# A fused FFT filter and top-128 FFN: the input laid out in DRAM in the order of the tile's rows, so that half of a batch is two transfers instead of eight

## The chip, the core and the metric

The kernel runs on one core of one Trainium2 chip. It is written in Bass under the Tile framework. The metric is device time in microseconds (us) for one execution. Five engines run their own instruction streams in order: TensorE (PE, matmuls; PEld is its weight load), VectorE (DVE), ScalarE (ACT), GpSimd (POOL) and SyncE (SP). In this kernel SP issues nearly all the transfers between DRAM and on-chip memory (SBUF); 16 DMA engines carry them out.

## The reference, cut to what matters

`x` has 8 batches of 3136 tokens with 256 channels, all in float32. The first half filters each channel along the tokens by a Fourier transform, a product with a complex filter and the inverse transform. The second half scores each token, takes the 128 best of each batch, runs them through a small two-layer network and adds the result, gated, to those tokens.

```
X = np.fft.rfft(x, axis=1)
y = np.fft.irfft(X * (filt_r + 1j * filt_i)[None], n=3136, axis=1)
scores = einsum('bsd,d->bs', y, w_gate); top 128 per batch
out = y;  out[top] += sigmoid(score) * (relu(y[top] @ w1) @ w2)
```

## The kernel before, in words

The 3136 tokens are taken as 98 x 32. A two-stage transform is used: an outer one over the 98 and an inner one over the 32, both as matmuls against constant tables.

The tile `X` has 128 partitions, 32 positions and 256 channels, and there is only one of it. A batch comes in folded for the outer transform: token row `a` (0 to 48) of the first and of the second half of the sequence, and even and odd positions (`w` = 0, 1), so that partitions 0 to 48 hold `w` = 0 and partitions 64 to 112 hold `w` = 1. Rows 49 to 63 belong to no token; the fold reads all 113 rows.

Work on a batch goes through these steps.

- `load` (line 535) brings a half of a batch (128 of the 256 channels) into `X`. For batches 0 and 1 it brings all 256 channels at once. Lines 542 and 545 issue it: four transfers of 48 partitions (first the two for partitions 64 to 111, then the two for partitions 0 to 47) and four of one partition.
- `outer` (line 404) works in 8 chunks of 32 channels, four to a half of `X`. For the batch that comes in, a chunk is folded (sum and difference, line 427, on POOL or DVE, or left to PE as extra matmuls), multiplied on PE (`amm`, line 453) and transposed into `UU` on DVE (line 457). The two letters of a chunk in `FOLD` say who makes the sum and who the difference: `p` POOL, `d` DVE, `x` PE.
- `inner` (line 341) makes the inner transform, the product with the filter and the inner inverse: lines 356 and 365 on PE, 374 and 390 on ACT, 378 on DVE, 381 on POOL.
- For the batch that goes out, `outer` transposes `UU` back on DVE (418), multiplies on PE (511) and copies the result over the same channels of `X` on ACT (514). When the four chunks of a half are done, `store` (533) writes this half to `out` in one transfer of 98 partitions; the last two batches use another path (489 to 498, stored by lines 528 and 531).
- `select` finds the 128 best tokens; it passes its scores through a scratch tensor in DRAM (`scr`, line 600, read back as `R`, line 605).

A half of `X` is thus reused in a fixed cycle: store of batch b, load of batch b + 3, fold and matmul of b + 3 in four chunks, results of batch b + 1 copied in, store of b + 1. While one batch comes in, the one before it is in the inner transform and the one before that goes out.

The order of all this is a list of numbers, `ORDER`, found beforehand with a planner: every step of the program is appended to `prog` by `op`, and the loop at the end issues them in the order of the list. Each engine keeps to that order, and SP too: a transfer is issued only when everything before it on SP has been issued. `PLAN` holds the other choices (`FOLD`, which engine spreads which part of the filter tables, which PSUM bank a matmul uses).

Of the kernel before, what the change touches and what calls it, by code (L numbers as in the profile page):

```python
# [44 lines left out]
def _tables(C):  # L45
# [45 lines left out]
    for r in range(8):  # L91
# [33 lines left out]
    BRING=["aazaaazz", "zvaaavzv", "aavaaaaa", "azvavaaa", "aaaaaaaa", "avzavvaa", "aaaaaaaa", "azvazavz"],  # L125
    SPR=[
        ["dve", "pool", "pool", "act"],
        ["pool", "dve", "pool", "pool"],
        ["dve", "act", "act", "dve"],
        ["dve", "act", "pool", "dve"],  # L130
    ],
    SELM=[0, 0, 0, 0, 0, 0, 0, 1],
    WPOOL=[7, 0, 1],
    PARTS=[(0, 2), (2, 4), (4, 8), (8, 13)],
    ALONE=[["a", "z", "v"], ["a"]],
    TRING=["z", "v", "z", "v"],
# [105 lines left out]
def kernel(  # L242
# [20 lines left out]
    HD = D // 2  # L263
    CW, CY = 32, 16
    DS = D + 1
    xv = x.rearrange("b (h a n w) d -> b w h a n d", h=2, w=2, n=N2 // 2)
    ov = out.rearrange("b (a c) d -> b a c d", c=N2)
    ow = out.rearrange("b (h a n w) d -> b w h a n d", h=2, w=2, n=N2 // 2)
    of = out.rearrange("b s d -> (b s) d")
# [841 lines left out]
```

## Time and profile before

| What | Value |
|---|---|
| median of 3 runs (lowest, highest) | 551.62 us (546.82, 552.71) |
| the profiled execution | 553.32 us, span of its instructions 551.5 us |
| TensorE clock granted in the span | 0.915 of full speed |
| PE busy | 458.5 us (83%) |
| DVE busy | 401.8 us (73%) |
| POOL busy | 291.8 us (53%) |
| ACT busy | 285.0 us (52%) |
| packets of the DMA queue that SP feeds | 103366, 62.53 MB, 61.8% of 16 engines' span |

Times in the rows below count from the first instruction of the profiled execution. A row of the timeline gives start, length, engine, line, operation, what it writes and reads, and in brackets how long its engine sat idle before it and what ended the idle time. [...]

### The profile page before, as it was taken

Reading aid. Unit: us, or ns where it says so; the run is one execution under the profiler, and the core shown is the slowest. Engines: PE = TensorE matmul, PEld = TensorE weight load, DVE = VectorE, ACT = ScalarE, POOL = GpSimd, SP = SyncE. Lnnn points to the kernel's source line nnn. Section 1 sums busy time; section 2 is a strip of 40 time slices with the busy share of each in tenths; the row PEclk is TensorE's granted clock in tenths of the full one; section 3 lists DMA queues with packets and bytes.
Section 4 is the critical chain, followed back from the end, with each engine's and each line's share of the span. In section 5 each row is a group of like instructions: output and inputs, shape, how many; then the busy total and the mean of one; then the engine's idle time right before and its main releaser. Section 6 shows DMA issues by size and latency. Waiting matters only on the chain. (4 is left out here: it accounts for less than half of the span.)

```text
span 551.5 us, 10702 instructions
## 1 busy us (share of the span) xinstructions
PE 458.5 (83%) x3888; PEld 232.9 (42%) x3888; DVE 401.8 (73%) x1016; ACT 285.0 (52%) x708; POOL 291.8 (53%) x236
## 2 busy tenths in 40 slices
PE   4094377799879989989799959996999896999996
PEld 4042153333324433434244415442443353566896
DVE  2086277779968998788579948994798897588642
ACT  1025242146565666458456835784467755776421
POOL 2092277695638735776378637854858334232022
PEclk9576878799999989989989988998899999799999
DMA  9999942860789385928883898289743336247410
GB/s 121 138 260 122 140 98 47 128 92 2 169 146 144 86 161 91 167 50 177 154 126 57 173 178 103 48 174 177 94 67 108 109 85 207 64 114 161 132 40 30
DMA packets 104186, 65.31 MB, mean 118 GB/s; under 512 B 5062, under 2 KB 102470, under 8 KB 103878
## 3 DMA queue, kind: packets, MB, share of 16 engines
q1 hardware_dynamic: 103366, 62.53, 61.8%
q0 software_dynamic: 768, 2.10, 1.2%
q8 instruction: 31, 0.51, 0.4%
q14 instruction: 21, 0.17, 0.1%
HBM read 37.68 MB, written 26.94 MB: 117 GB/s over the span
## 5 line engine op out<-in xcount | busy, mean ns | idle before, releaser
L381 POOL TENSOR_TENSOR q<-q,fb_sb 128x512 f32<-128x512 f32 (+1 forms) x104 | 133.0, 1298 | 82.5 <-ACT q L374 68.3
L427 POOL TENSOR_TENSOR s<-X 113x512 f32<-113x512 f32 x53 | 68.3, 1290 | 106.9 <-DMA X<-in_x_dram 59.7
L511 PE MATMUL py<-t,c_sb 128*98 128x512 f32 x208 | 119.0, 655 | 5.2 <-ACT X L514 3.9
L453 PE MATMUL pa<-X,c_sb 49*64 49x512 f32 x292 | 84.3, 708 | 27.3 <-DMA c_sb<-in_cst_dram 16.5
L396 DVE SCALAR_TENSOR_TENSOR rj<-pv,wg_sb 128x256 bf16<-128x256 f32 x200 | 83.8, 419 | 19.7 <-ACT UU L390 11.2
L457 DVE STREAM_TRANSPOSE UU<-pa 128x1024 f32<-128x1024 f32 x59 | 73.3, 1242 | 18.5 <-PE pa L453 17.8
L514 ACT COPY X<-py 98x512 f32<-98x512 f32 x104 | 60.5, 582 | 47.2 <-PE py L511 15.9
L418 DVE STREAM_TRANSPOSE t<-UU 128x1024 f32<-128x1024 f32 x64 | 78.5, 1229 | 5.3 <-PE py L511 3.7
L453 PE MATMUL pa<-s,c_sb 49*64 49x512 f32 x228 | 66.1, 650 | 18.0 <-POOL s L427 16.5
L374 ACT COPY q<-pz 128x512 f32<-128x512 f32 (+1 forms) x104 | 56.5, 586 | 47.3 <-PE pz L356 46.6
L365 PE MATMUL pv<-y,ti_sb 64*64 64x256 f32 x800 | 70.8, 395 | 11.0 <-DVE rj L396 11.0
L378 DVE TENSOR_TENSOR y<-pz,fa_sb 128x512 f32<-128x512 f32 (+1 forms) x104 | 67.9, 677 | 15.9 <-ACT q L374 13.4
L356 PE MATMUL pz<-UU,tf_sb 64*64 64x256 f32 x800 | 67.4, 426 | 13.2 <-DVE y L378 9.7
L390 ACT COPY UU<-pv 128x512 f32<-128x512 f32 x96 | 51.5, 588 | 46.8 <-PE pv L365 46.5
L365 PE MATMUL pv<-q,ti_sb 64*64 64x256 f32 x800 | 68.4, 384 | 3.0 <-POOL q L381 3.0
L427 POOL TENSOR_TENSOR X<-X 113x512 f32<-113x512 f32 x47 | 60.8, 1294 | 4.0 <-DVE s L427 0.6
L356 PEld LDWEIGHTS pz<-UU,tf_sb 64*64 64x64 f32 x800 | 32.0, 143 | 53.1 <-issue 20.6
L511 PEld LDWEIGHTS py<-t,c_sb 128*98 128x98 f32 x208 | 27.0, 170 | 54.4 <-ACT X L514 20.1
L365 PEld LDWEIGHTS pv<-y,ti_sb 64*64 64x64 f32 x800 | 30.5, 134 | 44.5 <-issue 13.1
L365 PEld LDWEIGHTS pv<-q,ti_sb 64*64 64x64 f32 x800 | 35.1, 136 | 16.3 <-POOL q L381 3.9
L453 PEld LDWEIGHTS pa<-X,c_sb 49*64 49x64 f32 x292 | 19.9, 148 | 40.8 <-issue 31.5
L427 DVE TENSOR_TENSOR s<-X 113x512 f32<-113x512 f32 x6 | 7.3, 1224 | 34.9 <-DMA fa_sb<-in_fri_dram 34.3
(193 smaller groups left out, 598.7 us busy)
## 6 DMA issues: line engine op xcount, KB each, us to landing
out_dram<-X SPq DMA_DIRECT2D x13, 1568.0 KB
X<-in_x_dram SPq DMA_DIRECT2D x48, 384.0 KB
X<-in_x_dram SPq DMA_DIRECT2D x8, 768.0 KB
out_dram<-X SPq DMA_DIRECT2D x12, 384.0 KB
R<-scr SPq DMA_DIRECT2D x16, 196.0 KB
fb_sb<-in_moe_w_dram SPq DMA_DIRECT2D x2, 1024.0 KB
ti_sb<-in_ti_dram SPq DMA_DIRECT2D x1, 832.0 KB
tf_sb<-in_tf_dram SPq DMA_DIRECT2D x1, 800.0 KB
```

The costliest lines, as they stand in the source:

```text
L356: nc.tensor.matmul(half(z, k)[o, hi], lhsT=tf_sb[p, l], rhs=urow(b, l, 0, D)[p], start=True, stop=True)
L365: nc.tensor.matmul(half(v, k)[o, j], lhsT=ti_at[p, t, i, hi], rhs=y[p, hi], start=t == 0, stop=t == 1)
L374: nc.scalar.copy(out=q[:np_], in_=half(h["z"], k)[:np_])
L378: nc.vector.tensor_tensor(out=y[:np_], in0=half(h["z"], k)[:np_], in1=fa_sb[:np_, i], op=ALU.mult)
L381: nc.gpsimd.tensor_tensor(out=h["q", k][:np_], in0=h["q", k][:np_], in1=fb_sb[:np_, i], op=ALU.mult)
L396: nc.vector.scalar_tensor_tensor(out=rj, in0=half(h["v"], k)[:, j], scalar=1.0, in1=wg_sb, op0=ALU.mult, op1=ALU.mult, accum_out=urow(b, l ...
L418: nc.vector.transpose(out=h["t"].rearrange("p d (l j) -> p d l j", j=2), in_=uchan(b_out, c))
L427: (nc.gpsimd if fold[k] == "p" else nc.vector).tensor_tensor(out=out, in0=two[0], in1=two[1], op=(ALU.add, ALU.subtract)[k])
L453: nc.tensor.matmul(a[o, w].rearrange("p (n d) -> p n d", d=CW), lhsT=lhs[p], rhs=rhs[p], start=n == 0, stop=n == len(terms) - 1)
L457: nc.vector.transpose(out=uchan(b_in, c), in_=h["a"].rearrange("p w (n d) -> p d n w", d=CW))
L511: nc.tensor.matmul(yp[:N1], lhsT=cc["wi"][:, :N1], rhs=h["t"][:, n * CY:(n + 1) * CY].rearrange("p a b -> p (a b)"), start=True, stop=True)
L514: nc.scalar.copy(out=X[:N1, :, at], in_=e["y"][:N1])
```

## The change

On the host, `x` is rearranged before the launch into an array of 8 batches x 2 halves of the channels x 113 rows x 32 positions x 128 channels, with zeros in rows 49 to 63. A half of a batch is then 113 rows of 16 KB, one after the other in DRAM, in the order of the tile's partitions. `load` becomes two transfers, one of 112 partitions and one of the last row, for every batch, the first two included. The two memsets that cleared rows 32 to 63 of `X` are gone. `ORDER` is another list, and some choices of `PLAN` differ.

```diff
-    nc.vector.memset(X[32:64, :N2 // 2], 0.0)
-    nc.gpsimd.memset(X[32:64, N2 // 2:], 0.0)
...
     def load(when, b, h, bias=0.0):
         def f():
-            if b >= B or (b < 2 and h == 1):
-                return
-            at = slice(0, D) if b < 2 else slice(h * HD, h * HD + HD)
-            for w in (1, 0):
-                for k in range(2):
-                    nc.sync.dma_start(out=Xh[64 * w:64 * w + 48, k, :, at], in_=xv[b, w, k, :48, :, at])
-            for w in range(2):
-                for k in range(2):
-                    nc.sync.dma_start(out=Xh[64 * w + 48:64 * w + 49, k, :, at], in_=xv[b, w, k, 48:49, :, at])
+            if b < B:
+                at = slice(h * HD, h * HD + HD)
+                nc.sync.dma_start(out=X[:112, :, at], in_=x[b, h, :112])
+                nc.sync.dma_start(out=X[112:RW2, :, at], in_=x[b, h, 112:])
...
+    xs = np.zeros((B, 2, RW2, 2, N2 // 2, D // 2), np.float32)
+    tokens = data["x"].reshape(B, 2, NH, N2 // 2, 2, 2, D // 2)
+    for w in range(2):
+        xs[:, :, 64 * w:64 * w + NH] = tokens[:, :, :, :, w].transpose(0, 4, 2, 1, 3, 5)
+    data["x"] = xs.reshape(B, 2, RW2, N2, D // 2)
...
-        "xx xd xx dp pp xx pp xx",
+        "xp dp pd dx dd pp xx pd",
...
-    1, 3, 0, 4, 2, 10, 35, 37, 46, 5, 47, 38, 42, 43, 11, 50, 6, 36, 39, 44, 15, 12, 48, 13, 51, 20, 40, 14, 52, 53,
```

Over the whole program the counts on the engines hardly differ: PE has two matmuls of `amm` more, DVE four folds more, POOL five fewer, the eight threshold steps of one batch's `select` go from ACT to DVE, and two subtractions of the network's weights from DVE to POOL.

Three places show how the order moves. The first is SP at the start of the program, up to the filter tables. Before:

```order
L542 DMA X<-in_x_dram 48x16x256 x4
L545 DMA X<-in_x_dram 1x16x256 x4
L1021 DMA c_sb<-in_cst_dram 128x192
L976 DMA fa_sb<-in_fri_dram 32x1024 x2
L976 DMA fb_sb<-in_fri_dram 32x1024 x2
L1024 DMA tf_sb<-in_tf_dram 128x1600
```

Now:

```order
L968 DMA fa_sb<-in_fri_dram 32x1024 x2
L968 DMA fb_sb<-in_fri_dram 32x1024 x2
L1013 DMA c_sb<-in_cst_dram 128x192
L536 DMA X<-in_x_dram 112x32x128
L537 DMA X<-in_x_dram 1x32x128
L536 DMA X<-in_x_dram 112x32x128
L537 DMA X<-in_x_dram 1x32x128
L1017 DMA wg_sb<-in_moe_w_gate_dram 128x256
L1016 DMA tf_sb<-in_tf_dram 128x1600
```

The first part of the filter tables (`fa_sb`, `fb_sb`) and the constants of `amm` (`c_sb`) now go ahead of the first batch, and the batch comes as two halves.

The second is SP in the middle of the program, from one store of a first half to the read-back of `select`, in the batch whose first half is stored fourth. Before:

```order
L533 DMA out_dram<-X 3136x1x128
L542 DMA X<-in_x_dram 48x16x128 x4
L545 DMA X<-in_x_dram 1x16x128 x4
L533 DMA out_dram<-X 3136x1x128
L600 DMA scr<-kf 98x2x32
L542 DMA X<-in_x_dram 48x16x128 x4
L545 DMA X<-in_x_dram 1x16x128 x4
L605 DMA R<-scr 128x1x392 x2
```

Now:

```order
L530 DMA out_dram<-X 3136x1x128
L536 DMA X<-in_x_dram 112x32x128
L537 DMA X<-in_x_dram 1x32x128
L592 DMA scr<-kf 98x2x32
L530 DMA out_dram<-X 3136x1x128
L536 DMA X<-in_x_dram 112x32x128
L537 DMA X<-in_x_dram 1x32x128
L597 DMA R<-scr 128x1x392 x2
```

The pair of store and load keeps its place; the scratch write of `select` stands ahead of the second store in this batch and in the two around it, where it stood behind it.

The third is PE at the start, from the first `amm` on (`pa`, `pz` and `pv` are PSUM tiles, `s` is a folded sum). Before:

```order
L453 MATMUL pa<-X,c_sb 64x512 x8
L453 MATMUL pz<-X,c_sb 64x512 x4
L453 MATMUL pz<-s,c_sb 64x512 x2
L453 MATMUL pv<-X,c_sb 64x512 x8
L453 MATMUL pa<-s,c_sb 64x512 x2
```

Now:

```order
L450 MATMUL pa<-X,c_sb 64x512 x8
L450 MATMUL pz<-s,c_sb 64x512 x2
L450 MATMUL pz<-X,c_sb 64x512 x2
L450 MATMUL pv<-s,c_sb 64x512 x2
L450 MATMUL pv<-X,c_sb 64x512 x2
```

The first batch has fewer chunks whose fold is left to PE, and PE begins with a chunk of the half that is loaded first.

## Rows read from the trace of the kernel before

**Rows 1.** The page's 40 slices of the span, 13.8 us each: the granted clock in tenths, and what the DMA engines moved.

```profile
PEclk9576878799999989989989988998899999799999
GB/s 121 138 260 122 140 98 47 128 92 2 169 146 144 86 161 91 167 50 177 154 126 57 173 178 103 48 174 177 94 67 108 109 85 207 64 114 161 132 40 30
```

**Rows 2.** The waits: engine, line and tile that waited, for what, us in total, times, the longest in us.

```profile
POOL s L427 <- DMA X<-in_x_dram: 59.7, 8, 13.4
```

**Rows 3.** The timeline of SP: issues of loads of `X` (L542) and of stores of a half (L533).

```profile
91.39 3.53 SPq L542 DMA_DIRECT2D X<-in_x_dram  x4
...
145.76 3.75 SPq L542 DMA_DIRECT2D X<-in_x_dram  x4
...
198.98 3.35 SPq L542 DMA_DIRECT2D X<-in_x_dram  x4
...
256.24 3.70 SPq L542 DMA_DIRECT2D X<-in_x_dram  x4
...
302.20 0.90 SPq L533 DMA_DIRECT2D out_dram<-X  x1
310.63 3.92 SPq L542 DMA_DIRECT2D X<-in_x_dram  x4
...
357.56 0.90 SPq L533 DMA_DIRECT2D out_dram<-X  x1
366.15 3.34 SPq L542 DMA_DIRECT2D X<-in_x_dram  x4
```

**Rows 4.** The timeline of POOL: the folds that waited for a load of `X`.

```profile
107.29 1.27 POOL L427 TENSOR_TENSOR s<-X 113x512 f32<-113x512 f32 x1 [4.67 <-DMA X<-in_x_dram]
161.25 1.26 POOL L427 TENSOR_TENSOR s<-X 113x512 f32<-113x512 f32 x1 [9.09 <-DMA X<-in_x_dram]
213.94 1.26 POOL L427 TENSOR_TENSOR s<-X 113x512 f32<-113x512 f32 x1 [6.02 <-DMA X<-in_x_dram]
...
270.38 1.25 POOL L427 TENSOR_TENSOR s<-X 113x512 f32<-113x512 f32 x1 [11.36 <-DMA X<-in_x_dram]
325.65 2.46 POOL L427 TENSOR_TENSOR s<-X 113x512 f32<-113x512 f32 x2 [13.43 <-DMA X<-in_x_dram]
...
380.14 1.25 POOL L427 TENSOR_TENSOR s<-X 113x512 f32<-113x512 f32 x1 [12.98 <-DMA X<-in_x_dram]
```

**Rows 5.** Stretches chosen for what the DMA engines carry in them: us, busy time of each engine (with its instructions), granted clock, share of the 16 DMA engines, GB/s. From 4 to 26 the load of batch 0; from 28 to 42 tables; from 359 to 365 a store of 98 partitions; from 368 to 377 one load of 4 transfers of 48 partitions, cut where its rate changes; from 450 to 454 a store as 4 transfers of 48 partitions; from 466 to 469 the network's weights onto 128 partitions, one of the two tensors in pieces of 1 KB.

```profile
4.00:26.00 22.00, 6.83 (x68) 6.69 (x68) 1.13 (x1) 0.20 (x1) 0.44 (x3) 0.72 1.14 140
28.00:42.00 14.00, 14.00 (x100) 6.53 (x100) 11.69 (x11) 3.48 (x3) 12.54 (x10) 0.77 0.89 255
...
359.00:365.00 6.00, 6.00 (x63) 2.75 (x63) 5.60 (x15) 5.02 (x15) 5.68 (x5) 1.00 0.91 257
368.00:369.00 1.00, 0.74 (x9) 0.13 (x2) 0.93 (x5) 0.97 (x4) 0.00 (x0) 1.00 1.10 244
369.00:373.00 4.00, 4.00 (x22) 1.26 (x22) 3.81 (x8) 2.89 (x9) 0.00 (x0) 1.00 1.23 136
373.00:374.00 1.00, 1.00 (x7) 0.41 (x3) 0.97 (x6) 0.26 (x2) 0.00 (x0) 1.00 1.22 195
374.00:377.00 3.00, 2.28 (x21) 0.85 (x20) 2.25 (x3) 2.33 (x7) 0.00 (x0) 1.00 1.25 143
...
450.00:454.00 4.00, 4.00 (x42) 1.85 (x38) 3.82 (x16) 1.89 (x4) 1.91 (x2) 1.00 0.86 182
...
466.00:469.00 3.00, 2.07 (x28) 1.75 (x32) 2.59 (x7) 1.56 (x5) 1.27 (x1) 0.80 1.03 373
```

**Rows 6.** The same view for stretches around the waits of rows 4: the first number after the stretch's length is PE's busy time, the third from the end the granted clock.

```profile
330.00:385.00 55.00, 50.33 (x427) 21.52 (x421) 42.86 (x117) 33.87 (x91) 35.41 (x29) 0.93 0.71 126
...
262.00:274.00 12.00, 8.47 (x48) 2.71 (x42) 7.97 (x17) 6.58 (x20) 3.54 (x3) 0.97 0.85 135
274.00:281.00 7.00, 7.00 (x34) 2.47 (x35) 2.96 (x8) 2.21 (x7) 6.84 (x7) 0.57 0.49 138
316.00:329.00 13.00, 6.99 (x36) 2.05 (x36) 6.28 (x11) 6.16 (x19) 3.27 (x3) 0.96 1.09 198
329.00:336.00 7.00, 7.00 (x43) 2.67 (x43) 2.91 (x8) 2.48 (x8) 6.25 (x6) 0.59 0.12 25
372.00:382.00 10.00, 5.85 (x37) 1.98 (x36) 5.66 (x10) 5.21 (x16) 1.78 (x2) 1.00 1.08 186
382.00:390.00 8.00, 7.49 (x30) 2.20 (x26) 3.35 (x8) 1.82 (x5) 7.84 (x7) 0.57 0.27 79
...
152.00:166.00 14.00, 11.19 (x80) 3.94 (x71) 8.99 (x22) 9.06 (x27) 4.75 (x5) 0.93 0.89 151
...
100.00:111.00 11.00, 7.63 (x38) 3.23 (x42) 7.99 (x20) 1.00 (x4) 6.18 (x6) 0.62 0.77 117
```

**Rows 7.** The timeline at the start: the first `amm`, the first matmul of `inner`, and the first `amm` of batch 1.

```profile
27.92 3.93 PE L453 MATMUL pa<-X,c_sb 49*64 49x512 f32 x16 [16.54 <-DMA c_sb<-in_cst_dram]
...
45.82 1.99 PE L356 MATMUL pz<-UU,tf_sb 64*64 64x256 f32 x16 [3.31 <-DVE UU L457]
...
70.65 4.48 PE L453 MATMUL pa<-X,c_sb 49*64 49x512 f32 x16 [9.34 <-DMA X<-in_x_dram]
```

**Rows 8.** The groups by line: busy us in all, mean ns of one, idle time before them and what ended it.

```profile
L427 POOL TENSOR_TENSOR s<-X 113x512 f32<-113x512 f32 x53 | 68.3, 1290 | 106.9 <-DMA X<-in_x_dram 59.7 <-DMA c_sb<-in_cst_dram 23.3 <-DMA fa_sb<-in_fri_dram 11.6
L427 DVE TENSOR_TENSOR s<-X 113x512 f32<-113x512 f32 x6 | 7.3, 1224 | 34.9 <-DMA fa_sb<-in_fri_dram 34.3 <-POOL s L427 0.7
L284 DVE MEMSET X<- 32x4096 f32 x1 | 3.5, 3472 | 1.7 <-PEq L1100 1.7
```

More of the change, by code (lines that the diff above doesn't have):

```diff
@@ L124 @@
     BACK=["ffffffff", "ffffffff", "ffffffff", "ffffffff", "ffffffff", "ffffffff", "qeqeqqqe", "eeeeffff"],
-    BRING=["aazaaazz", "zvaaavzv", "aavaaaaa", "azvavaaa", "aaaaaaaa", "avzavvaa", "aaaaaaaa", "azvazavz"],
+    BRING=["aazaavza", "vaazvzav", "vazzzaza", "zzavazza", "aaaaaava", "avzvvvaz", "aaaaaaaa", "azvaaaaa"],
     SPR=[
-        ["dve", "pool", "pool", "act"],
-        ["pool", "dve", "pool", "pool"],
-        ["dve", "act", "act", "dve"],
+        ["dve", "act", "pool", "pool"],
+        ["act", "pool", "act", "dve"],
         ["dve", "act", "pool", "dve"],
+        ["act", "act", "pool", "dve"],
     ],
-    SELM=[0, 0, 0, 0, 0, 0, 0, 1],
-    WPOOL=[7, 0, 1],
+    SELM=[0, 0, 0, 0, 0, 1, 0, 1],
+    WPOOL=[4, 5, 0, 1, 7],
     PARTS=[(0, 2), (2, 4), (4, 8), (8, 13)],
     ALONE=[["a", "z", "v"], ["a"]],
-    TRING=["z", "v", "z", "v"],
+    TRING=["z", "z", "v", "z"],
     URING=["m", "v", "v"],
@@ L265 @@
     DS = D + 1
-    xv = x.rearrange("b (h a n w) d -> b w h a n d", h=2, w=2, n=N2 // 2)
     ov = out.rearrange("b (a c) d -> b a c d", c=N2)
@@ L519, in outer @@
             if b_out >= 0 and o + CW == HD:
-                op(t0 + 4.4, "sp", 7.2, lambda hx=hx: store(b_out, hx),
+                op(t0 + 4.4, "sp", 7.2 if back == "f" else 10.5, lambda hx=hx: store(b_out, hx),
                    [("x", hx, c - k) for k in range(HD // CW)], [("out", b_out)], lat=.9)
@@ L536, in f @@
         def f():
-            if b >= B or (b < 2 and h == 1):
-                return
-            at = slice(0, D) if b < 2 else slice(h * HD, h * HD + HD)
-            for w in (1, 0):
-                for k in range(2):
-                    nc.sync.dma_start(out=Xh[64 * w:64 * w + 48, k, :, at], in_=xv[b, w, k, :48, :, at])
-            for w in range(2):
-                for k in range(2):
-                    nc.sync.dma_start(out=Xh[64 * w + 48:64 * w + 49, k, :, at], in_=xv[b, w, k, 48:49, :, at])
+            if b < B:
+                at = slice(h * HD, h * HD + HD)
+                nc.sync.dma_start(out=X[:112, :, at], in_=x[b, h, :112])
+                nc.sync.dma_start(out=X[112:RW2, :, at], in_=x[b, h, 112:])
         n = HD // CW
-        op(when, "sp", 6.8 if 2 <= b < B else 12.5 if b < 2 and h == 0 else .01, f, (), [("x", h, c) for c in range(h * n, h * n + n)], lat=2, bias=bias)
+        op(when, "sp", 6.8 if b < B else .01, f, (), [("x", h, c) for c in range(h * n, h * n + n)], lat=2, bias=bias)
     def select(T0, b, st):
```

193 rows, old and new, of tables (FOLD, ORDER) are left out of this document.

## The prediction, made before the changed kernel was run

> **What bounds the kernel now.** I read the slices of the page first: the granted clock is low in slices 2 to 8 and dips again in slices 15, 18, 21, 24, 25, 28 and 29, the last four of these beside peaks of the DMA rate (173 to 178 GB/s) [rows 1]. The view of the waits names one large one: POOL's fold waits for the load of `X`, 59.7 us over 8 times [rows 2]. The timelines of SP and POOL give the load its length. From the issue of a first half to the fold that waited for it pass 15.5, 15.0, 14.1, 15.0 and 14.0 us for batches 3 to 7, mean 14.7, and 15.9 us for batch 2 [rows 3, 4]. The store ahead of it needs 8.43 and 8.59 us from its issue to the issue of the load that waits for it [rows 3], for the same bytes: 98 rows of 16 KB, 1.61 MB. So the cycle of a half of `X` is 8.5 + 14.7 us before the fold begins, and PE does not have that much other work.
>
> What that costs is in the windows [rows 6]. From 316 to 329 PE is busy 6.99 of 13 us, and in the next 7 us it runs at a granted clock of 0.59: having idled, it comes back at the lower of its two levels. The same stands at 262 to 281 and 372 to 390. Between these places PE is close to full: 50.33 of 55 us from 330 to 385, the slow 8 us included.
>
> Why a load is slower than a store, the DMA windows show [rows 5]. The store of 98 partitions in one transfer moves 257 GB/s. The load begins at 244 in its first microsecond, then runs at 136 and 143, with 195 only in the microsecond in which it passes from partitions 64 to 111 to partitions 0 to 47. The load of batch 0, whose pieces are 1 KB instead of 512 B, has the same 140, so it is not a price per piece. Reading DRAM is not the limit either: the weights, partly in 1 KB pieces, come at 373 onto 128 partitions. And a store cut in the same way, four times 48 partitions, falls to 182. What goes with the low rate is that one transfer's 48 partitions lie in one half of the tile.
>
> [...]
>
> **The change part by part.** *The length of a load.* Now 112 partitions in one transfer, with 15 rows of zeros more: 113 x 16 KB = 1.85 MB. I price it by the store, the nearest row: 1.61 MB at 257 GB/s is 6.2 us, which leaves 2.3 us at its two ends; 1.85 MB at 257 is 7.2, and 9.5 us with the ends. Bounds: 8.5 us, if the zero rows cost nothing; and 14.7 x 1.85 / 1.61 = 16.9, if it keeps its rate. A loss is thus not excluded. I take 9.5, 5.2 less than today, because the store has the same rows and the same 512 B pieces, the other way round.
>
> *Loads in the middle (batches 3 to 7).* A load 5.2 us shorter gives back PE's idle time up to 5.2 us, and the slow clock behind it if the idle time goes [rows 6]. At 316: 5.2 of 6.0 idle, and 7 x 0.41 = 2.9 of clock, 8.1. At 372: 4.2 + 0.5 idle and 8 x 0.43 = 3.4, 8.1. At 262: 3.5 and 7 x 0.43 = 3.0, 6.5. At 152: 2.8 and 14 x 0.07 = 1.0, 3.8. For the load folded at 213.94 I count nothing. **Sum 26 us.** What is late next is PE itself: a batch's PE work is about 47 us at full clock (50.33 less the 3.4), against a cycle of 55.
>
> *Start.* The stretch up to batch 1's first matmul at 70.65 [rows 7] is DMA alone: two batches of `X`, 6.42 MB, at 140 take 45.9; the tables and constants, 5.6 MB by their shapes, at 255 [rows 5] take 22.0; with the 2.3 this gives 70.2. Now 7.41 MB at 257 take 28.8, and the sum is 53.1. The order must let PE follow. The first `amm` stands at 27.92 and `inner` begins at 45.82. Now 0.6 MB of tables (2.4 us), then halves of 7.2 us each and the 2.3: the first half is in at 12, the second at 19, so `inner` begins by about 37. PE was through its work ahead of batch 1's `amm` at 61.3 (70.65 less 9.34), 15.5 us after `inner` began; that is 52.5 now. **Gain 17 us.**
>
> *Batch 2.* Its load is 6.4 us shorter (15.9 to 9.5). From 100 to 111 PE idles 3.4 us and loses 11 x 0.38 = 4.2 to the clock [rows 6]; since DVE is busy there too (8.0 of 11), I count 5.
>
> *Edits at nothing.* The memsets (3.5 us on DVE [rows 8], one of the same size on POOL) end before any load now or then; without them the first load need not wait, but tables are ahead of it. Four folds more on DVE are 4.9 us and five fewer on POOL 6.5 [rows 8], spread over the batches, on engines with idle time in each; if DVE were full they would cost those 4.9. The threshold steps on DVE and the two weight subtractions lie off the chain of the middle. SP issues 2 transfers instead of 8 (the four larger ones alone take 3.3 to 3.9 us [rows 3]), which nobody waits for but the read-back of `select`. The scratch write ahead of the second store makes that store wait for `select`'s keys in three batches, and the load behind it too; the folds that waited in rows 4 are all of first halves, so I count 0, up to 2 us a batch if the keys are late.
>
> Sum 26 + 17 + 5 = 48. The profiled execution took 553.3, so 505.3; the median of the runs is 1.7 lower, so **504 us**.
>
> **The rivals.**
> 1. *Another wait takes the place in the middle.* The load lands early, but the fold then meets POOL and DVE (42.86 of 55 us busy [rows 6]) out of step, or the second store sits behind the moved scratch write. For it: DVE has little room, and every engine keeps to its list. Against: the load is the only large wait of rows 2. Only a third of the 26 returns: 504 + 17 = 521.
> 2. *The load stays at its rate, and is slower.* Place: the write of 512 B pieces into a strided tile. If a load runs at 140 whatever partitions it spans, each takes 16.9 us, 2.2 more for six loads, 13 us, and the start takes 52.9 + 22.0 + 2.3 = 77.2, 6.5 later: 551.6 + 20 = 571. It decides where the load falls under 1.85 MB / (14.7 - 2.3 us) = 149 GB/s. For it: no load of `X` in the trace holds more than 143 for long. Against: the 195 at the seam, and the 257 of the store.
> 3. *No net change.* The load is faster, but the new order loses what it gains: 546 to 557. For it, only that the list is altogether new.
>
> **How the numbers follow.** Forecast 0.70, rival 1 0.15, rival 2 0.08, rival 3 0.07. Low end: all idle and slow clock of rows 6 returned, 32, the start 22 (both halves of batch 1 in before PE asks, with `inner` never waiting for tables) and batch 2 with 7, 61 in all: 491; a little lower if the load takes 8.5, 486. High end: a load half-way between 9.5 and 14.7 gives half of the 48, 528; with rival 1 inside, 530. The range of 486 to 530 holds the forecast's case and rival 1, about 0.8 after the tails. One per cent, 5.5 us, is about what these runs can tell from no change (they spread from 546.8 to 552.7). Faster 0.85, within it 0.07, slower 0.08.
>
> **What would show it.** From the issue of a load to the fold, 9 to 10 us; 240 GB/s and more while it runs; POOL's wait for `X` under 20 us in all; first `amm` near 12 and `inner` near 37; batch 1's `amm` near 53; stores of first halves 48 to 50 us apart instead of 55, with the clock at 1.00 through them. The forecast is wrong if loads stay near 140 GB/s, or if they are fast and the stores remain 55 us apart.

## The result and the profile after

The changed kernel takes 506.69 us (median of 4 runs, 501.60 to 507.52) against 550.91 (4 runs) for the kernel before on the same chip: ratio 0.919 with a 95% interval of [0.911, 0.927], **faster**. The profiled execution took 506.0 us, span 504.3.

The slices of the changed kernel's page, PE's granted clock and the DMA rate, against [rows 1]:

```profile
PEclk9687898999999999999999999999999989999999
GB/s 202 249 257 231 101 147 98 86 10 192 194 181 127 173 64 204 111 208 66 193 116 201 78 202 93 209 113 195 163 1 101 76 144 173 128 125 114 92 44 33
```

The dips of the clock in the middle are gone. The first four slices move 202 to 257 GB/s; before, three of them moved 121 to 138. POOL's waits of the changed kernel (total us, times, longest):

```profile
POOL s L424 <- DMA X<-in_x_dram: 76.2, 12, 10.4
```

This sum has grown from 59.7 [rows 2], though each load is shorter: the waits for first halves of batches 3 to 7 fell from 52.9 to 38.0, those for second halves rose from 2.2 to 23.9, and 14.4 at the start wait for batch 0 (before, 4.7 for batch 2). The timelines of SP and POOL in the changed kernel, one store and the load behind it:

```profile
311.78 0.88 SPq L530 DMA_DIRECT2D out_dram<-X  x1
320.17 0.62 SPq L536 DMA_DIRECT2D X<-in_x_dram  x1
320.83 6.16 SPq L537 DMA_DIRECT2D X<-in_x_dram  x1
...
331.73 1.29 POOL L424 TENSOR_TENSOR s<-X 113x512 f32<-113x512 f32 x1 [8.76 <-DMA X<-in_x_dram]
```

The load's issue waits 8.39 us for the store as before [rows 3]; from it to the fold pass 11.6 us, where [rows 3, 4] had 15.0. The five first halves of batches 3 to 7 take 10.9, 11.1, 11.5, 11.8 and 11.6 us, mean 11.4 (14.7 before). Their second halves (11.9 to 12.4) are now all waited for by POOL as well (before only two of them, for about 1 us each).

PE in the changed kernel around that load (windows; length, PE busy, ..., granted clock third from the end), against [rows 6]:

```profile
312.00:318.00 6.00, 5.10 (x50) 1.79 (x42) 4.31 (x15) 1.66 (x3) 5.92 (x6) 1.00 0.73 204
318.00:325.00 7.00, 7.00 (x61) 3.16 (x61) 6.43 (x18) 6.47 (x20) 2.43 (x2) 1.00 0.72 174
325.00:332.00 7.00, 6.79 (x41) 2.27 (x33) 6.37 (x19) 5.04 (x15) 0.27 (x1) 1.00 0.64 149
332.00:339.00 7.00, 6.96 (x54) 2.56 (x55) 5.97 (x13) 4.98 (x14) 6.84 (x6) 1.00 0.35 95
```

While POOL stands (0.27 of 7 us busy) PE works: 6.79 of 7 us, at clock 1.00 then and after. The place that lost 6 us to idle time and 2.9 to the clock now loses 0.25 us of idle time between 318 and 339, and nothing to the clock.

The granted clock has two values in both traces, 1.00 and 0.50; a stretch that holds both shows a mean. The kernel before at that place, while PE is idle, behind the idle time, and then:

```profile
323.00:327.50 4.50, 0.00 (x0) 0.00 (x0) 1.15 (x2) 1.10 (x5) 1.85 (x2) 1.00 0.95 261
328.50:334.50 6.00, 6.00 (x27) 1.95 (x24) 2.13 (x7) 1.36 (x5) 5.90 (x5) 0.50 0.11 29
335.00:340.00 5.00, 5.00 (x62) 2.94 (x64) 4.41 (x16) 2.54 (x9) 2.50 (x2) 1.00 1.08 138
```

The changed kernel's start, PE's timeline against [rows 7] (first `amm`, `inner`, first `amm` of batch 1):

```profile
14.96 1.93 PE L450 MATMUL pa<-X,c_sb 49*64 49x512 f32 x5 [8.34 <-DMA X<-in_x_dram]
...
35.63 1.13 PE L353 MATMUL pz<-UU,tf_sb 64*64 64x256 f32 x8 [4.17 <-DVE UU L454]
...
53.41 1.19 PE L450 MATMUL pa<-X,c_sb 49*64 49x512 f32 x4
```

I cut each kernel in three at its stores of first halves: **start** (up to the first of them, batch 0's), **middle** (to the sixth, batch 5's), **tail** (to the end). Windows over the middle and the tail, of the kernel before

```profile
136.79:411.56 274.77, 248.37 (x2114) 104.17 (x2110) 222.40 (x587) 165.90 (x434) 172.91 (x139) 0.94 0.71 127
411.56:551.50 139.94, 123.92 (x1002) 83.11 (x994) 99.01 (x293) 78.68 (x207) 47.28 (x41) 0.97 0.39 104
```

and of the changed one:

```profile
111.42:356.86 245.44, 231.67 (x2063) 98.97 (x2055) 212.39 (x563) 160.06 (x416) 157.64 (x126) 1.00 0.60 152
356.86:504.26 147.40, 128.45 (x1028) 85.71 (x1020) 104.93 (x325) 77.49 (x192) 54.24 (x47) 0.97 0.38 99
```

The start is 25.4 us shorter, the middle 29.3, the tail 7.5 longer: 47.2. PE's idle time in the middle fell from 26.4 to 13.8 us, its clock rose from 0.94 to 1.00, and it holds 51 matmuls fewer; the tail holds 26 more and the start 29.

### The profile page after: what moved, and what is told of

It is laid out like the page before. It is cut to its first block, busy times and chain, and to the rows that moved or that the text cites. A ratio compares the mean times of both kernels' runs of the same rounds, so it can differ in the third digit from the quotient of the medians.

```text
span 504.3 us, 10483 instructions
## 1 busy us (share of the span) xinstructions
PE 443.7 (88%) x3892; PEld 227.7 (45%) x3892; DVE 398.9 (79%) x1040; ACT 283.5 (56%) x686; POOL 284.8 (56%) x231
## 3 DMA queue, kind: packets, MB, share of 16 engines
q1 hardware_dynamic: 62278, 66.46, 52.5%
## 4 chain that ended last, share of the span: by engine, by line
PE 38%; DMA 23%; DVE 13%; POOL 12%; issue 6%; SPq 4%; ACT 3%; POOLq 0%; DVEq 0%; ACTq 0%
DMA X<-in_x_dram 16%; PE py L508 9%; PE pv L362 8%; PE pa L450 5%; DMA out_dram<-X 5%; POOL q L378 5%; PE pz L353 4%; POOL s L424 4%; DVE rj L393 4%; POOL X L424 3%; SPq L537 2%; DVE y L375 2%; DVE UU L454 2%; PE pa L907 1%; PE pv L877 1%
## 5 line engine op out<-in xcount | busy, mean ns | idle before, releaser
L508 PE MATMUL py<-t,c_sb 128*98 128x512 f32 x208 | 113.9, 629 | 6.3 <-ACT X L511 5.6
L424 POOL TENSOR_TENSOR s<-X 113x512 f32<-113x512 f32 x52 | 68.1, 1315 | 76.8 <-DMA X<-in_x_dram 76.2
L450 PE MATMUL pa<-X,c_sb 49*64 49x512 f32 x332 | 80.6, 641 | 15.1 <-DMA X<-in_x_dram 9.2
L375 DVE TENSOR_TENSOR y<-pz,fa_sb 128x512 f32<-128x512 f32 (+1 forms) x104 | 67.4, 674 | 10.9 <-ACT q L371 10.4
L353 PE MATMUL pz<-UU,tf_sb 64*64 64x256 f32 x800 | 62.3, 410 | 14.5 <-DVE y L375 7.9
L371 ACT COPY q<-pz 128x512 f32<-128x512 f32 (+1 forms) x104 | 56.4, 586 | 28.7 <-PE pz L353 24.4
L450 PE MATMUL pa<-s,c_sb 49*64 49x512 f32 x220 | 59.4, 612 | 2.9 <-DVE UU L454 2.0
L424 POOL TENSOR_TENSOR X<-X 113x512 f32<-113x512 f32 x43 | 56.2, 1309 | 5.8 <-DVE s L424 3.4
L353 PEld LDWEIGHTS pz<-UU,tf_sb 64*64 64x64 f32 x800 | 29.1, 136 | 49.6 <-issue 16.3
L508 PEld LDWEIGHTS py<-t,c_sb 128*98 128x98 f32 x208 | 25.8, 163 | 51.4 <-ACT X L511 18.8
L616 ACT ACTIVATE junk<-R,nb 128x392 bf16<-128x392 f32 x48 | 29.9, 623 | 4.9 <-DVE nb L635 4.3
```

The costliest lines, as they stand in the source:

```text
L353: nc.tensor.matmul(half(z, k)[o, hi], lhsT=tf_sb[p, l], rhs=urow(b, l, 0, D)[p], start=True, stop=True)
L371: nc.scalar.copy(out=q[:np_], in_=half(h["z"], k)[:np_])
L375: nc.vector.tensor_tensor(out=y[:np_], in0=half(h["z"], k)[:np_], in1=fa_sb[:np_, i], op=ALU.mult)
L424: (nc.gpsimd if fold[k] == "p" else nc.vector).tensor_tensor(out=out, in0=two[0], in1=two[1], op=(ALU.add, ALU.subtract)[k])
L450: nc.tensor.matmul(a[o, w].rearrange("p (n d) -> p n d", d=CW), lhsT=lhs[p], rhs=rhs[p], start=n == 0, stop=n == len(terms) - 1)
L508: nc.tensor.matmul(yp[:N1], lhsT=cc["wi"][:, :N1], rhs=h["t"][:, n * CY:(n + 1) * CY].rearrange("p a b -> p (a b)"), start=True, stop=True)
```

## The experiments

My theory, **P**: a transfer into 48 partitions of one half of the tile is slow, one that spans both halves is fast. Rivals: **O**, the new order of issue makes the gain; **C**, a partition's 16 KB lying together in DRAM; **N**, the number of transfers; **S**, the length of the pieces in DRAM. Load lengths below are from issue to the fold that waited, mean over the loads of batches 3 to 7 that were waited for (changed kernel: 10 loads, 11.8 us).

### Either half of the change alone

*order_only* is the changed kernel with `x` in its old order and the two memsets back:

```diff
-                nc.sync.dma_start(out=X[:112, :, at], in_=x[b, h, :112])
-                nc.sync.dma_start(out=X[112:RW2, :, at], in_=x[b, h, 112:])
+                for w in (1, 0):
+                    for k in range(2):
+                        nc.sync.dma_start(out=Xh[64 * w:64 * w + 48, k, :, at], in_=xv[b, w, k, :48, :, at])
...
```

> The changed kernel's order of issue, fold table and rings, but x in its old order in DRAM and the half of X loaded as before, by four transfers of 48 partitions and four of one row (both halves of batches 0 and 1 apart). Theory P (a transfer whose partitions lie in one half of the tile is slow, and the change gains by spanning both halves): the loads keep 136 to 150 GB/s and 14 to 16 us from issue to fold, first inner later than 43 us, and the whole lies between 540 and 575 us, so that the order alone gains little or loses. Rival O (the gain comes from the new order): 505 to 525 us with loads as slow as before.

*layout_only* is the kernel before with the new `x` and the two lines marked `-` above, both halves of batches 0 and 1 in one step.

> The kernel before with its own order, fold table and rings, and only the new order of x in DRAM with its load of 112 partitions and one row. Theory P: loads take 11 to 12.5 us from issue to fold, and most of the 45 us comes: 503 to 522 us, the first number if the order before ends its last 100 us as it did (139.9 us from the last store of a first half to the end, against 147.4 in the changed kernel). Rival O: within 10 us of the kernel before, 540 to 555 us.

order_only: 542.7 us, ratio 0.984 [0.980, 0.989]. layout_only: 511.0 us, 0.930 [0.922, 0.939]. Windows over the middle of order_only:

```profile
117.50:394.90 277.40, 249.43 (x2063) 103.83 (x2055) 212.21 (x563) 160.39 (x415) 156.44 (x125) 0.93 0.71 126
```

and of layout_only:

```profile
116.20:366.60 250.40, 236.55 (x2114) 100.72 (x2110) 221.55 (x587) 165.63 (x434) 175.58 (x141) 0.99 0.58 149
```

With the order alone the middle is no shorter than before, PE idle for 28.0 us and its clock at 0.93, with loads of 15.1 us; with the layout alone it is 24.4 us shorter: 12.6 of idle time and, at the same 2114 matmuls, 11.8 of busy time, which goes with the clock's rise from 0.94 to 0.99. So O falls for the middle. For the start it doesn't: order_only reaches its first store at 117.5 us, layout_only at 116.2, both together at 111.4, before 136.8. Either half of the change gets most of it. PE in order_only (first matmul of `inner`, first `amm` of batch 1):

```profile
41.14 1.98 PE L356 MATMUL pz<-UU,tf_sb 64*64 64x256 f32 x16 [3.03 <-DVE UU L457]
...
59.27 1.20 PE L453 MATMUL pa<-X,c_sb 49*64 49x512 f32 x4
```

layout_only came out as expected. order_only, of which I expected little or nothing, gains 1.6% by its interval, and begins `inner` at 41.1 us, not later than 43; what it wins at the start it partly loses in its tail (151.3 us). Its profiled execution took 548.1 us, 5.4 above its median; if all of that lay in the middle, the middle would still be 272.0 us, 2.8 shorter than before.

Since both made a gain, I ran the changed kernel and layout_only side by side.

> The changed kernel itself, unaltered, beside the three others: 501 to 509 us, ratio to the kernel before 0.911 to 0.927 as in its first runs.

> The kernel before with the new layout and load alone, once more, to compare with the changed kernel on the same chip. If the new order of issue adds something to the layout: 3 us or more slower than the changed kernel in this call (509 to 514 us). If the order is worth nothing beside the layout: within 2 us of the changed kernel.

503.9 us, 0.916 [0.913, 0.920], and 509.8 us, 0.926 [0.922, 0.930]: on top of the layout the order is worth 5.9 us. By the windows of these two it gains 3.9 us in the start and 8.8 in the middle and loses 7.0 in the tail.

### What in the load is fast

Both kernels here read the new `x` with six transfers; *cut_by_partitions* goes back to 48 partitions (and has the memsets again), *cut_by_positions* keeps 112:

```diff
 cut_by_partitions
+                for w in (1, 0):
+                    for k in range(2):
+                        nc.sync.dma_start(out=Xh[64 * w:64 * w + 48, k, :, at], in_=x[b, h, 64 * w:64 * w + 48, 16 * k:16 * k + 16])
+                for w in range(2):
+                    nc.sync.dma_start(out=X[64 * w + 48:64 * w + 49, :, at], in_=x[b, h, 64 * w + 48:64 * w + 49])
 cut_by_positions
+                for k in range(4):
+                    nc.sync.dma_start(out=X[:112, 8 * k:8 * k + 8, at], in_=x[b, h, :112, 8 * k:8 * k + 8])
+                for k in range(2):
+                    nc.sync.dma_start(out=X[112:RW2, 16 * k:16 * k + 16, at], in_=x[b, h, 112:, 16 * k:16 * k + 16])
```

> The changed kernel, its x in DRAM in the new order, but each half of X loaded by four transfers of 48 partitions x 16 positions (64 to 111 twice, then 0 to 47 twice) and two of one row. Theory P: 136 to 150 GB/s but for the seam, 14 to 16 us from issue to fold, 540 to 575 us for the whole. Rival C (the new order in DRAM, by which a partition's 16 KB lie together, is what made it faster): loads 11 to 12.5 us, 505 to 515 us.

> The changed kernel, but each half of X loaded by four transfers of 112 partitions x 8 positions and two pieces of the one row: as many transfers as in the kernel cut by partitions. Theory P: 220 GB/s and more, 11 to 13 us from issue to fold, 503 to 515 us. Rival N (the number of transfers in the queue costs, each with its own start and end): 14 to 16 us from issue to fold, 540 to 575 us.

532.1 us and 496.9 us, one run each, the latter again as cut_by_positions_2:

> The kernel cut by positions (496.9 us in one run) again, for an interval: 494 to 500 us and a ratio to the kernel before of 0.895 to 0.908 if the gain over the changed kernel (506.7) is real; 502 to 509 if that one run was a stray.

499.9 us, 0.903 [0.896, 0.910], with loads of 10.9 us in the first of the two runs. The cut by positions is thus below the 503 to 515 us that I expected of it, and stays there. *pitched* leaves the changed kernel's two transfers and lays whole 1 KB positions into DRAM (`x[b, :112, :, at]`), so that the pieces are 512 B again.

> The changed kernel and its two transfers, but x lies in DRAM with whole positions of 1 KB, so that half of X reads 512 B of every 1 KB, as the kernel before did, now onto 112 partitions at once. Theory P alone (only the partitions that a transfer spans count): 220 to 250 GB/s, 11 to 12 us from issue to fold, 503 to 511 us. Rival S (the length of the pieces that lie together in DRAM counts as well: 15.0 us with 512 B in the kernel with the order alone, 13.6 us with 8 KB in the one cut by partitions): 12.6 to 14 us, 513 to 530 us.

503.3 us, 0.912 [0.905, 0.919], loads of 11.4 us. Windows of 5 us inside a load of the middle, in this order: order_only, cut_by_partitions, the changed kernel, cut_by_positions, pitched (last column GB/s):

```profile
300.00:305.00 5.00, 5.00 (x27) 1.64 (x25) 4.40 (x13) 3.74 (x12) 0.00 (x0) 1.00 1.23 143
```

```profile
292.00:297.00 5.00, 5.00 (x32) 1.83 (x26) 4.90 (x12) 3.51 (x10) 0.00 (x0) 1.00 1.24 139
```

```profile
272.00:277.00 5.00, 5.00 (x27) 1.87 (x27) 4.49 (x12) 3.97 (x12) 0.00 (x0) 1.00 1.03 247
```

```profile
265.50:270.50 5.00, 5.00 (x38) 1.88 (x32) 4.90 (x13) 3.21 (x9) 0.46 (x1) 1.00 1.13 245
```

```profile
273.00:278.00 5.00, 5.00 (x30) 1.84 (x26) 4.74 (x12) 3.77 (x11) 0.00 (x0) 1.00 1.18 261
```

The rate follows the partitions that one transfer spans and nothing else that was varied: 139 and 143 GB/s with 48, whether the DRAM side is new or old; 245 to 261 with 112, in two transfers or six, in long pieces or 512 B. Windows of 5 us in the other loads of these runs give 134 to 155 and 226 to 268. C, N and S fall for the rate. One rival stands: no run separates the number of the partitions (48 against 112) from their lying in one half of the tile or in both. For the halves speaks the 195 of [rows 5], in the microsecond in which the load passes from one half to the other. cut_by_partitions missed its expectation in time all the same: loads of 13.7 us, not 14 to 16, and 532.1 us, 10.6 under order_only (one run). Its rate is order_only's within a few per cent, so the difference lies at the load's ends; SP issues the six transfers in 6.1 us and order_only's eight in 8.1. Whether the fewer issues or the DRAM side make it, no run separates.

### What else stands in the load

In the changed kernel SP spends 6.16 us on the issue of the one row behind the large transfer (timeline above). *row_first* swaps the two lines; *cut_row_first* puts the row ahead of the four transfers by positions; *whole128* pads `x` with zero rows to 128 and uses a single transfer, `out=X[:, :, at], in_=x[b, h]`.

> The changed kernel, but the transfer of the one row (partition 112) is issued ahead of that of 112 partitions. In the changed kernel SP spends 5.5 to 8 us on the issue of the row behind the large transfer, and the row's pieces land last. Theory R (the row ends the load): issue to fold falls from a mean of 11.8 us to 9.8 to 10.8, and the whole from 506.7 to 497 to 503 us. Rival: the large transfer's own last packets end the load, 11.4 to 12.0 us as now, 504 to 509 us.

> The changed kernel with the row's transfer first and then four transfers of 112 partitions x 8 positions. Theory R (the late row is what the single transfer loses): as good as the kernel cut by positions or up to 4 us better, 491 to 498 us, issue to fold 9.5 to 10.6 us. Rival (the cut itself gains, by an earlier start of the data, and the row is hidden): 495 to 499 us, the same as cut by positions, 10.3 to 11.4 us from issue to fold.

> The kernel with the row first and four transfers by positions, once more beside the changed kernel: 493 to 500 us, 7 to 13 us faster than the changed kernel in this call, if it beats both kernels; 502 or more if it does not.

> The changed kernel with x padded with zeros to 128 rows and half of X loaded by one transfer of 128 partitions, 2.10 MB, and no transfer of a row. By the rate of the changed kernel (245 GB/s) the data take 1.0 us more than 1.85 MB and the late row is gone: 10 to 11.5 us from issue to fold, 497 to 505 us. [...]

row_first: 501.2 us, 0.909 [0.902, 0.916], which overlaps the changed kernel's interval; 11.2 us from the issue of the large transfer to the fold, between the 9.8 to 10.8 and the 11.4 to 12.0 that the two sides expected. The row explains about 0.6 us of a load, no more. SP's timeline in row_first:

```profile
109.49 0.99 SPq L530 DMA_DIRECT2D out_dram<-X  x1
110.59 5.31 SPq L536 DMA_DIRECT2D X<-in_x_dram  x1
118.91 0.60 SPq L537 DMA_DIRECT2D X<-in_x_dram  x1
```

The row's issue is as long behind the large store (5.31 us), but there SP would wait for the store anyway.

cut_row_first: 496.6 us, 0.900 [0.894, 0.907], loads of 10.1 us from the first of the four. The time fits both sides of its expectation, the load the first (9.5 to 10.6). Beside the changed kernel (503.9 us, 0.916 [0.913, 0.920]) it takes 499.1 us, 0.908 [0.905, 0.911]. The intervals don't touch: it beats the kernel before and the changed one, though by 4.8 us and not the 7 to 13 that I expected. whole128, in the same company: 499.3 us, 0.906 [0.902, 0.910], no different from it, loads of 10.9 us. Windows inside a load of whole128:

```profile
123.00:128.00 5.00, 4.76 (x24) 1.55 (x22) 4.97 (x11) 2.80 (x10) 0.00 (x0) 1.00 1.03 306
```

(and 295 from 267 to 272 us.) Its rate lies above the 245 GB/s that I reckoned with, its load and its time within the expectation (10 to 11.5 and 497 to 505 us): 14% more bytes than in 112 rows come in no more time (10.9 us against row_first's 11.2), so the added rows of zeros cost nothing that shows.

## Why the prediction was right, and where not

Forecast 504 us, range 486 to 530; measured 506.7, and 503.9 when run again. The mechanism holds: that the loads were slow for the partitions that one transfer spans is shown by the cut kernels (139 GB/s with 48, 245 with 112), the middle's gain by layout_only; what in the chip makes such a transfer slow, no run shows. That the whole came so near (48 us forecast, 47.2 in the spans) is luck: start and middle gave 6.7 more than forecast, and the tail took 7.5 that was priced at nothing. Step by step:

- **The load's length was mis-sized**: 9.5 us forecast, 11.4 measured for the first halves. The rate was right (257 taken from the store; 234 to 261, mean 249, in windows of 5 us of the ten loads, 2.7 us after the issue). The 2.3 us at the two ends, carried over from the store, were not: 1.85 MB at 249 GB/s take 7.4, so the ends take 4.0. Most of the missing 1.7 lies at the load's end. By windows of 0.1 us, from the moment when 98% of a load's bytes have moved, 1.9 to 2.5 us pass to the fold in the changed kernel (four first halves), 1.4 to 1.9 in row_first, and 0.8 to 1.6 from a store's 98% to the next issue on SP (two stores of the kernel before, five of the changed one). The late row is about 0.6 of it; why the load's last pieces come so late without it, no run shows.
- **The middle, 26 forecast, 29.3 measured.** The rows behind the 26 hold 16.2 of idle time and 10.3 of clock. layout_only, which keeps the order, shows 12.6 and 11.8 (9.3 and 11.9 in its second execution): less idle time returned, as a load shrank by 3 to 4 and not by 5.2 us, and a little more of the clock. The order adds 5.0 (8.8 between the second executions), with 51 matmuls that it takes out of the middle (231.67 us / 2063 = 0.11 us each, 5.7 us). That part is moved, not gained. The sum came near with two sizes off in opposite directions.
- **Start and batch 2, 22 forecast, 25.4 measured** to the first store. `amm` at 14.96 instead of "near 12", `inner` at 35.63 ("by about 37"), batch 1's `amm` at 53.41 ("near 53"). But the bytes over the rate, on which the 17 us rested, did not set batch 1's start. In the changed kernel batch 1's `amm` follows PE's own work with no idle time before it, and no fold of batch 1 waited for its load; what set it is the work on batch 0 that stands ahead of it on PE, the leg that the prediction put at 52.5, and not the 53.1 of the bytes. order_only shows the same: its loads keep 143 GB/s, its batch 1 `amm` stands at 59.27 where the bytes give 70.2, and it gains 19.3 by the first store. I had named the order only as a condition ("The order must let PE follow"), and it moves the start as much as the rate does.
- **The tail, 0 forecast, 7.5 lost**, and 4.6 in the second execution of the changed kernel (144.6 us). It comes with the order: layout_only has 142.0 and, again, 137.6. Of the 7.5, 4.5 are PE's busy time, with 26 matmuls more behind the sixth store (0.125 us each, 3.2 us), and 2.9 are idle time. So a good part of it is the other end of what the middle gave away; what makes the idle time was not tried. The edits that I priced at nothing I looked at one by one, and missed that a new list shifts work from stage to stage.
- **A sign was wrong**: POOL's wait for `X` was to fall under 20 us and rose to 76.2 (58.7 in the second execution, against 59.7 before). A fold that stands at the head of POOL's list waits as long as POOL is early, whether PE needs it or not: from 325 to 332 us POOL was busy 0.27 of 7 us and PE 6.79. PE's idle time and clock are the sign to look at; there the forecast held (clock 1.00 from 111 to 357 us, stores 49.1 us apart on average, 48 to 50 forecast).
- Rival 1 (a new wait in the middle) is what POOL's waits look like, but PE doesn't follow. Rival 2 needed a load under 149 GB/s; it has 247. Rival 3 fell with the time.
- The range's low end counts 32 us for the idle time and slow clock of [rows 6]; the stretches there hold 17.0 and 11.2, together 28. The low end would be 490, which changes nothing here.

What is next: in the middle PE is busy 231.7 of 245.4 us at full clock. The faster loads of cut_row_first shorten it only to 238.8, with 9.2 us idle (window of its second profile below). PE bounds this stage now, as the prediction named it.

```profile
109.30:348.10 238.80, 229.63 (x2063) 99.18 (x2057) 212.07 (x563) 160.20 (x416) 159.37 (x128) 1.00 0.64 156
```

## What to carry to other kernels

In these runs the rate of a transfer of `X` went with the partitions that it spans (134 to 155 GB/s with 48, 226 to 268 with 112, 295 and 306 with 128), and not with the number of transfers or the length of the pieces in DRAM. So before lengthening the pieces, try to lay the data so that each transfer covers the whole tile; the zero rows that filled it cost nothing here (loads of 10.9 us with 128 rows, 11.2 with 113). Cut along the positions afterwards: that gained another 4.8 us with the row first. Find the evidence in the kernel's own other transfers, here the store with the same bytes and the jump of the rate where the transfers pass from one half to the other. And after the change read the engine that sets the end: POOL's waits for `X` grew here from 59.7 to 76.2 us, while PE's idle time in the middle fell from 26.4 to 13.8. Look for work that a new order moves across the lines at which you cut the time into stages: here it took 51 matmuls out of the middle, and the tail held 26 more.

## What the hardware showed beside that

- The issue of a 16 KB transfer of one partition behind the 1.84 MB one holds SP for 5.5 to 8.0 us in the changed kernel (median 6.2 of 16); the single transfer of whole128 is issued in 0.6 us (median).
- Four transfers of a quarter of the positions each are no slower than one (245 to 268 GB/s in windows of 5 us against 226 to 261); the first `amm` of the kernel starts at 10.1 us in cut_by_positions instead of 15.0, as it reads the first 16 positions first.
